# Hash masks in an attention kernel: 64 bucket features per token in place of 12 bit features

## The chip, the cores and the metric

The kernel runs on one core of one Trainium2 chip. The metric is the device time of one execution in microseconds. The kernel before took 825.91 us (median of three executions, 824.48 to 827.63).

## What is computed

Sixteen (batch, head) pairs of attention over 768 tokens with head size 64, followed by two dense blocks on the 1536 x 512 result. The attention is masked by a hash: each token gets six bits, the signs of its products with six random directions, and a query sees only the keys that have the same six bits.

```
q_bits = (einsum('bhsd,dk->bhsk', q, proj) > 0)      # proj: 64 x 6; the same for k
mask   = q_bucket[:, :, :, None] == k_bucket[:, :, None, :]
scores = where(mask, scale * q @ k.T, -1e9)
attn   = softmax(scores);  out = attn @ v
x = ((x @ w1) * (x @ w2)) @ w3 @ w_out
out = (sigmoid(x @ w_gate) * (x @ w_val)) @ w_out2
```

A row of `scores` in which no key has the query's bits is -1e9 everywhere, so its softmax is uniform.

## The kernel before

The weights of the dense blocks arrive as 64-bit floats and are turned into 32-bit ones on the chip (`decode`, lines 323 to 343, on ACT, POOL and DVE). Matrix products are made from values that are split in a high and a low part.

**Attention.** A head has six groups (`NT`) of 128 queries, 96 groups (`NG`) in all. For a group `emit_qk` (lines 453 to 463) makes scores of 128 x 768 in one of two PSUM tiles (`scs`), by four products of 384 columns. The contraction has 128 rows: in the second pair of products (`aq`, `ak`, line 463) rows 0 to 63 hold the token's numbers and rows 64 to 127 its mask features. `emit_max` (lines 465 to 471) takes the negated maximum with one reduction into a spare PSUM column beside the scores (line 470), and then makes a pair (scale, bias) with a second instruction (line 471): the pair is (1, -max), or (0, 0) where the maximum is below -0.5 x BIG, that is where all keys are masked. `emit_exp` (line 481) applies `Exp` with that scale and that bias as operands by partition. `emit_T` transposes the result on TensorE (line 514), copies and splits it (lines 517, 519), `emit_av` multiplies by v (line 532).

**Mask features.** `prep(h)` prepares the next head: POOL scales and splits q and k (lines 398 to 400), `hashes` (lines 380 to 386) makes the hash sums by three products of 384 columns in one tile of the PSUM ring `psT` (four tiles, shared with the transposes, the products with v and the filler), for each half of the tokens, and DVE turns them into features with one instruction (line 407). Three DMAs then put the features where the products want them. In the matrix `pq` the directions stand twice, with either sign, for q and for k, so a bit gives two features, 12 in all, and a mismatch in any bit adds at least -BIG = -2^33 to the score. `first_head` (lines 418 to 448) does the same for head 0 on ACT and DVE, with the threshold on line 446.

**Filler and order.** Work of the dense blocks that needs no attention result (`gen_fill`, `gen_first`, with the decoding) is spread between the groups. The order on each engine is then set by `order_engines`: a list schedule over priorities and its own costs, in which PE, ACT, DVE, POOL and SP each get one fixed order of instructions. That order can therefore differ on every engine wherever an instruction is added, removed or costs something else. What follows the attention (`moe`) is in program order and outside this plan.

**Setup.** Lines 800 to 817 fill the constants before the first products: identity, `pq`, thresholds (`thr`), the limit (`lim`) and a one beside the scores.

Of the kernel before, what the change touches and what calls it, by code (L numbers as in the profile page):

```python
# [10 lines left out]
F32 = mybir.dt.float32  # L11
F32R = mybir.dt.float32r
U32 = mybir.dt.uint32
I32 = mybir.dt.int32
U64 = mybir.dt.uint64
AF = mybir.ActivationFunctionType
ALU = mybir.AluOpType
AX = mybir.AxisListType

BIG = float(2 ** 33)  # L20
TINY = 2.0 ** -126


F64_LO = 2.0 ** -15
# [205 lines left out]
def lsh_attention_moe_moe2_kernel(  # L230
# [20 lines left out]
    B, H, S, D = v.shape  # L251
    P = 128
    NB = proj.shape[1]
    NT = S // P
    HS = S // 2
# [13 lines left out]
    act = nc.scalar  # L269
    dve = nc.vector  # L270
    pool = nc.gpsimd
    pe = nc.tensor
# [5 lines left out]
    def f(ap):  # L278
        return ap.bitcast(F32)

    cst = Tiles(ctx.enter_context(tc.tile_pool(name="cst", bufs=1, side="left")), "cst", 1)
# [4 lines left out]

    idf = cst.tile([P, P], F32, name="idf")
    pq_raw = cst.tile([P, NB], F32, name="pq_raw")
    pq = [cst.tile([P, P], F32R, name=f"pq{i}") for i in range(2)]
    thr = cst.tile([P, 2], F32, name="thr")  # L290
    scl = cst.tile([P, 1], F32, name="scl")
    lim = cst.tile([P, 2], F32, name="lim")

    xall = big.tile([P, KC, NTOK], F32, name="xall")
    xraw = [xall[:, :, i * CH:(i + 1) * CH] for i in range(NSW)]
# [84 lines left out]
    def hashes(m, half):  # L380

        hs = slice(half * HS, (half + 1) * HS)
        ps = psT.tile([P, 512], F32, tag="t", name="gps")
        for n, (w, x) in enumerate(((0, "aq"), (0, "bq"), (1, "aq"))):
            pe.matmul(ps[:, :HS], lhsT=pq[w], rhs=m[x][:, hs], start=n == 0, stop=n == 2)
        return ps

    def prep(h):
# [75 lines left out]

    def emit_max(g):
        s = sc_t[g]
        one = s[:, 0, HS:HS + 2]
        b = ap_.tile([P, 2], F32, tag="sm", name=f"sm{g}", bufs=4)
        sm_t[g] = b
        dve.tensor_reduce(out=one[:, 1:2], in_=s[:, :, :HS], op=ALU.max, axis=AX.XY, negate=True)  # L470
        dve.scalar_tensor_tensor(out=b, in0=lim, scalar=one[:, 1:2], in1=one, op0=ALU.is_gt, op1=ALU.mult)  # L471

    def emit_exp(g):
        h, t = divmod(g, NT)
        s = sc_t.pop(g)
        sm = sm_t.pop(g)
        if t == 0:
            su_t[h] = ap_.tile([P, NT], F32, tag="su", name=f"su{h}")
        e = ap_.tile([P, S], F32, tag="e", name=f"e{g}", bufs=4)
        e_t[g] = e  # L480
        act.activation(  # L481
            out=e.rearrange("p (a c) -> p a c", a=2), in_=s[:, :, :HS], func=AF.Exp,
            bias=sm[:, 1:2], scale=sm[:, 0:1], accum_out=su_t[h][:, t:t + 1],
        )
        if t == NT - 1:
            emit_rows(h)
# [310 lines left out]
    start = first_head()  # L797
    next(start)
    make_identity(nc, idf)
    o = D // 2  # L800
    for t in pq:
        dve.memset(f(t), 0.0)
    for r, c0, sg in ((slice(0, D), D, 1.0), (slice(D, P), 0, -1.0)):
        for b0, sgn in ((c0, sg), (c0 + o, -sg)):
            hi, lo = (t[r, b0:b0 + NB] for t in pq)
            dve.tensor_scalar(out=hi, in0=pq_raw[r], scalar1=sgn, scalar2=None, op0=ALU.mult)
            dve.scalar_tensor_tensor(out=lo, in0=pq_raw[r], scalar=sgn, in1=f(hi), op0=ALU.mult, op1=ALU.subtract)
    dve.memset(thr[D:P, 1:2], -BIG)
    dve.memset(thr[0:D, 1:2], 1.0)
    dve.memset(thr[:, 0:1], 0.0)  # L810
    for t in scs:
        dve.memset(t[:, 0, HS:HS + 1], 1.0)
    dve.memset(lim, 0.5 * BIG)
    dve.memset(scl[0:D], SCALE)
    dve.memset(scl[D:P], 1.0)
    dve.memset(thr[0:o, 0:1], -TINY)
    dve.memset(thr[D + o:P, 0:1], -TINY)
    next(start)
    fill = gen_fill()
    first = gen_first()  # L820
# [113 lines left out]
```

## Time and profile before

| | |
|---|---|
| median of three executions | 825.91 us (824.48 to 827.63) |
| the profiled execution | 825.27 us, span 823.4 us |
| busy share of the span | PE 96%, weight loads 80%, DVE 63%, ACT 60%, POOL 45% |
| instructions | PE 3984, DVE 870, ACT 912, POOL 378 |
| `Exp` (L481) | first at 13.8 us, last at 347.0 us |
| granted TensorE clock, mean | 0.994 |

The span begins with the first instruction; 1.9 us of the execution lie outside it. Up to about 366 us the attention is done together with the filler; behind it stands the dense work. Matmuls are pipelined and their ends are modelled, so the busy share of PE is larger than the share of the time in which it takes in columns.

### The profile page before, as it was taken

The numbers are of one execution on the slowest core, as the hardware profiler recorded it, in microseconds if no ns is written. First come the engines' busy times: TensorE is split into PE (matmuls) and PEld (weight loads), VectorE is DVE, ScalarE is ACT, GpSimd is POOL, SyncE is SP. The second block draws the span as 40 slices with busy tenths as digits, with TensorE's granted clock in tenths as the row PEclk, the third lists the DMA queues.
The fourth block names the chain that finished last, engine by engine and source line by source line (L and its number), as shares of the span: only waits on it lengthen the run. The fifth ranks groups of instructions, "written<-read, shape, count | busy, mean of one in ns | idle before, by whom it ended". The sixth has DMA issues, their size and how long they took to land.

```text
span 823.4 us, 11452 instructions
## 1 busy us (share of the span) xinstructions
PE 787.2 (96%) x3984; PEld 657.4 (80%) x3984; DVE 516.2 (63%) x870; ACT 494.3 (60%) x912; POOL 367.9 (45%) x378
## 2 busy tenths in 40 slices
PE   5799899899899999979999999999999999999998
PEld 4577788798788998868888888888888888888886
DVE  7669999887899889976654545686722222222222
ACT  5689777776787876875444645656534333343332
POOL 4567655645466553267243434445432323232320
PEclk9999999999999999999999999999999999999999
DMA  7856656424456443230021213334101000010001
GB/s 248 212 166 175 195 162 174 109 81 122 122 148 173 122 107 98 79 112 27 26 77 52 77 51 112 119 106 151 52 1 51 1 1 0 1 52 0 1 1 51
DMA packets 28585, 74.45 MB, mean 90 GB/s; under 512 B 6128, under 2 KB 8432, under 8 KB 28528
## 3 DMA queue, kind: packets, MB, share of 16 engines
q1 hardware_dynamic: 28528, 73.73, 30.4%
q8 instruction: 31, 0.51, 0.3%
q14 instruction: 26, 0.21, 0.1%
HBM read 52.83 MB, written 3.19 MB: 68 GB/s over the span
## 4 chain that ended last, share of the span: by engine, by line
PE 74%; DVE 12%; ACT 5%; POOL 3%; issue 3%; DMA 3%; SPq 0%; ACTq 0%; POOLq 0%; DVEq 0%
PE m L692 18%; PE pa L692 18%; PE pb L692 17%; PE av L532 5%; PE tp L514 4%; PE p L692 3%; PE wacc L587 3%; DVE s L470 3%; DVE pt L519 2%; PE s L460 2%; DVE da L338 2%; PE s L463 2%; ACT e L481 2%; PE y L692 1%; DMA qk<-in_qk_dram 1%
## 5 line engine op out<-in xcount | busy, mean ns | idle before, releaser
L732 DVE TENSOR_TENSOR pb<-pb,a 128x512 f32<-128x512 f32 x52 | 36.3, 698 | 163.6 <-PE pb L692 157.1
L481 ACT ACTIVATE e<-s,sm 128x768 f32<-128x768 f32 x96 | 95.5, 995 | 25.5 <-DVE sm L471 25.0
L514 PE MATMUL tp<-idf,e 128*128 128x128 f32 x576 | 103.6, 276 | 1.4 <-DVE xall L545 0.7
L692 PE MATMUL pa<-x,wah 128*128 128x512 f32 x320 | 100.2, 395 | 4.5 <-ACT wah L276 4.5
L336 POOL TENSOR_SCALAR da<-da 128x512 f32<-128x512 f32 x76 | 50.7, 668 | 114.2 <-ACT da L334 109.0
L692 PE MATMUL pb<-x,wbh 128*128 128x512 f32 x320 | 99.8, 391 | 0.0
L686 POOL TENSOR_TENSOR wal<-xall,wah 128x512 fp32r<-128x512 f32 x36 | 46.8, 1301 | 118.4 <-ACT wah L276 117.8
L470 DVE TENSOR_REDUCE s<-s 128x1 f32<-128x768 f32 x96 | 91.6, 956 | 11.7 <-PE s L463 9.0
L517 ACT ACTIVATE pt<-tp 128x512 fp32r<-128x512 f32 (+1 forms) x144 | 81.8, 597 | 14.3 <-PE tp L514 13.3
L532 PE MATMUL av<-pt,spv 128*128 128x256 f32 (+1 forms) x576 | 86.4, 300 | 1.4 <-DVE pt L519 1.2
L519 DVE TENSOR_TENSOR pt<-tp,pt 128x512 fp32r<-128x512 f32 x126 | 82.8, 680 | 6.2 <-ACT pt L517 6.0
L532 PEld LDWEIGHTS av<-pt,spv 128*128 128x128 f32 (+1 forms) x576 | 73.6, 185 | 12.1 <-DVE pt L519 4.0
L514 PEld LDWEIGHTS tp<-idf,e 128*128 128x128 f32 x576 | 72.8, 142 | 11.0 <-DVE ft L407 1.5
L334 ACT ACTIVATE da<-st 128x512 f32<-128x512 f32 x76 | 50.9, 670 | 48.2 <-DVE w1r L343 18.0
L460 PE MATMUL s<-bk,bq 128*128 128x384 f32 x192 | 62.0, 381 | 15.9 <-ACT e L481 13.2
L692 PEld LDWEIGHTS pa<-x,wah 128*128 128x128 f32 x320 | 60.7, 190 | 18.3 <-ACT wah L276 4.9
L692 PEld LDWEIGHTS pb<-x,wbh 128*128 128x128 f32 x320 | 60.3, 189 | 12.7 <-ACT wbh L276 0.2
L587 PE MATMUL wacc<-wo,t 128*128 128x512 f32 x192 | 66.9, 423 | 1.3 <-POOL t L575 0.7
L692 PE MATMUL pa<-x,wal 128*128 128x512 f32 x160 | 62.8, 393 | 0.0
L338 DVE SCALAR_TENSOR_TENSOR da<-st,da 128x512 uint32<-128x512 uint32 x76 | 62.1, 821 | 1.0
L692 PE MATMUL pb<-x,wbl 128*128 128x512 f32 x160 | 62.6, 391 | 0.0
L463 PE MATMUL s<-ak,aq 128*128 128x384 f32 x192 | 60.6, 379 | 0.0
(137 smaller groups left out, 1797.5 us busy)
## 6 DMA issues: line engine op xcount, KB each, us to landing
st<-in_moe_w_dram SPq DMA_DIRECT2D x32, 512.0 KB, 3.9
st<-in_moe_w_out_dram SPq DMA_DIRECT2D x20, 512.0 KB, 3.5
st<-in_moe_w_gate_dram SPq DMA_DIRECT2D x12, 512.0 KB, 3.3
st<-in_moe_w_val_dram SPq DMA_DIRECT2D x12, 512.0 KB, 3.3
qk<-in_qk_dram SPq DMA_DIRECT2D x15, 384.0 KB, 4.4
rr<-row SPq DMA_DIRECT2D x16, 192.0 KB, 3.4
out_dram<-o SPq DMA_DIRECT2D x12, 256.0 KB, 2.0
ak<-aq SPq DMA_DIRECT2D x15, 192.0 KB, 2.5
```

The source lines that it names most:

```text
L334: act.activation(out=f(a), in_=f(hw), func=AF.Abs)
L338: dve.scalar_tensor_tensor(out=a, in0=hw, scalar=0xC0000000, in1=a, op0=ALU.bitwise_and, op1=ALU.bitwise_or)
L460: pe.matmul(s[:, half, :HS], lhsT=m["bq"][:, qs], rhs=m["bk"][:, ks], start=True, stop=False)
L463: pe.matmul(s[:, half, :HS], lhsT=m["aq"][:, qs], rhs=m["ak"][:, ks], start=False, stop=True)
L470: dve.tensor_reduce(out=one[:, 1:2], in_=s[:, :, :HS], op=ALU.max, axis=AX.XY, negate=True)
L481: act.activation(out=e.rearrange("p (a c) -> p a c", a=2), in_=s[:, :, :HS], func=AF.Exp, bias=sm[:, 1:2], scale=sm[:, 0:1], accum_out=su_ ...
L514: pe.transpose(ps[:, i * P:(i + 1) * P], e_t[g - g % 2 + a][:, c * P:(c + 1) * P], idf)
L517: act.activation(out=dh, in_=src, func=AF.Copy)
L519: dve.tensor_tensor(out=d, in0=src, in1=f(dh), op=ALU.subtract)
L532: pe.matmul(acc[:w.shape[1], :2 * P].rearrange("p (a t) -> p a t", a=2), lhsT=w, rhs=r[:, :, c], start=(c == 0 and i == 0), stop=(c == NT ...
L587: pe.matmul(acc, lhsT=t3[x][:, j], rhs=wo[y][:, j], start=(j == 0 and n == 0), stop=(j == NF1 - 1 and n == 2))
L692: mm = pe.matmul(ps, lhsT=lhs[x], rhs=rhs[y], start=start and n == 0, stop=stop and n == 2)
```

## The change

The features become 64 per token, one for each bucket. The hash sums of q and k go to separate rows (0 to 31 and 32 to 63) of a 64-row product; ACT takes their signs into a new tile `sg`; a further product with the constant pattern `pat` (plus and minus one by the bits of the bucket's number) adds up the agreements; the thresholds on lines 407 and 446 turn the sum into 1 for the own bucket of q, and into -BIG for each other bucket of k. A key with another hash then adds exactly one -BIG = -2^60, and a score beside it vanishes by rounding, so in a fully masked row all scores are equal. The reduction writes the negated maximum straight to SBUF, the second instruction (line 471) is gone, and `Exp` takes the scale as the constant 1.

```diff
-BIG = float(2 ** 33)
-TINY = 2.0 ** -126
+BIG = float(2 ** 60)
...
-    pq = [cst.tile([P, P], F32R, name=f"pq{i}") for i in range(2)]
+    pq = [cst.tile([P, D], F32R, name=f"pq{i}") for i in range(2)]
...
-    lim = cst.tile([P, 2], F32, name="lim")
+    zb = cst.tile([D, 1], F32, name="zb")
+    pat = cst.tile([D, P], F32R, name="pat")
+    bits = [cst.tile([D, P], I32, name=f"bits{i}") for i in range(2)]
...
         for n, (w, x) in enumerate(((0, "aq"), (0, "bq"), (1, "aq"))):
-            pe.matmul(ps[:, :HS], lhsT=pq[w], rhs=m[x][:, hs], start=n == 0, stop=n == 2)
+            pe.matmul(ps[0:D, :HS], lhsT=pq[w], rhs=m[x][:, hs], start=n == 0, stop=n == 2)
+        sg = ap_.tile([D, HS], F32R, tag="sg", name="sg")
+        act.activation(out=sg, in_=ps[0:D, :HS], func=AF.Sign, scale=2.0 ** 64, bias=zb)
+        pe.matmul(ps[:, :HS], lhsT=pat, rhs=sg, start=True, stop=True)
         return ps
...
-        one = s[:, 0, HS:HS + 2]
-        b = ap_.tile([P, 2], F32, tag="sm", name=f"sm{g}", bufs=4)
+        b = ap_.tile([P, 1], F32, tag="sm", name=f"sm{g}", bufs=4)
         sm_t[g] = b
-        dve.tensor_reduce(out=one[:, 1:2], in_=s[:, :, :HS], op=ALU.max, axis=AX.XY, negate=True)
-        dve.scalar_tensor_tensor(out=b, in0=lim, scalar=one[:, 1:2], in1=one, op0=ALU.is_gt, op1=ALU.mult)
+        dve.tensor_reduce(out=b, in_=s[:, :, :HS], op=ALU.max, axis=AX.XY, negate=True)
...
-            bias=sm[:, 1:2], scale=sm[:, 0:1], accum_out=su_t[h][:, t:t + 1],
+            bias=sm, scale=1.0, accum_out=su_t[h][:, t:t + 1],
...
+    pool.iota(bits[0], pattern=[[0, 2], [1, D]], base=0, channel_multiplier=0)
+    for r in range(0, D, o):
+        pool.iota(bits[1][r:r + o], pattern=[[0, P]], base=0, channel_multiplier=1)
+    dve.memset(zb, -2.0 ** -64)
...
-    for r, c0, sg in ((slice(0, D), D, 1.0), (slice(D, P), 0, -1.0)):
-        for b0, sgn in ((c0, sg), (c0 + o, -sg)):
-            hi, lo = (t[r, b0:b0 + NB] for t in pq)
-            dve.tensor_scalar(out=hi, in0=pq_raw[r], scalar1=sgn, scalar2=None, op0=ALU.mult)
-            dve.scalar_tensor_tensor(out=lo, in0=pq_raw[r], scalar=sgn, in1=f(hi), op0=ALU.mult, op1=ALU.subtract)
...
+    dve.tensor_tensor(out=bits[0], in0=bits[0], in1=bits[1], op=ALU.logical_shift_right)
+    dve.tensor_scalar(out=bits[0], in0=bits[0], scalar1=1, scalar2=None, op0=ALU.bitwise_and)
+    dve.memset(f(pat), 0.0)
+    for r, c, sg in ((slice(0, o), slice(D, P), 2.0), (slice(o, D), slice(0, D), -2.0)):
+        dve.tensor_scalar(out=pat[r, c], in0=bits[0][r, c], scalar1=sg, scalar2=-0.5 * sg, op0=ALU.mult, op1=ALU.add)
+    for r, c in ((slice(0, D), 0), (slice(D, P), o)):
+        hi, lo = (t[r, c:c + NB] for t in pq)
+        dve.tensor_copy(hi, pq_raw[r])
+        dve.tensor_tensor(out=lo, in0=pq_raw[r], in1=f(hi), op=ALU.subtract)
```

## Rows read from the trace of the kernel before

**Rows 1.** Windows by stage: length, then busy us (instructions) of each engine, granted clock, DMA.

```profile
0.00:14.00 14.00, 5.17 (x14) 4.06 (x14) 8.31 (x30) 6.62 (x10) 3.80 (x10) 1.00 0.75 238
14.00:60.00 46.00, 38.30 (x195) 29.71 (x195) 32.01 (x54) 34.20 (x66) 30.59 (x39) 0.96 0.71 199
60.00:350.00 290.00, 278.43 (x1754) 244.55 (x1753) 265.07 (x473) 230.21 (x451) 155.93 (x178) 0.99 0.49 134
...
400.00:823.40 423.40, 419.76 (x1822) 341.94 (x1820) 178.92 (x278) 196.04 (x338) 149.10 (x130) 1.00 0.14 48
```

**Rows 2.** Chain that ended last, 60 to 350 us, shares by line (cut by the view).

```profile
by line: PE av L532 11.6%; PE tp L514 8.4%; PE wacc L587 7.6%; DVE s L470 7.0%; DVE pt L519 6.5%; issue 5.9%; PE p L692 5.1%; PE s L460 4.5%; PE s L463 4.3%; DVE da L338 4.1%; ACT e L481 2.9%; PE gps L385 2.8%; DVE w3f L343 2.1%; DVE da L33
```

**Rows 3.** Waits of the span: who waited for whom, us in total, times, longest.

```profile
ACT e L481 <- DVE sm L471: 25.0, 24, 5.6
...
PEld s L460 <- ACT e L481: 19.2, 19, 3.4
...
PE s L460 <- ACT e L481: 13.2, 10, 3.1
```

**Rows 4.** Groups by line and form, DVE: busy us, mean ns, idle before, releasers.

```profile
L407 DVE TENSOR_SCALAR ft<-gps,thr 128x384 fp32r<-128x384 f32 x30 | 20.1, 672 | 11.4 <-PE gps L385 11.0
L471 DVE SCALAR_TENSOR_TENSOR sm<-lim,s 128x2 f32<-128x2 f32 x96 | 20.0, 209 | 0.9
```

**Rows 5.** The same view from 60 to 350 us, DVE.

```profile
L471 DVE SCALAR_TENSOR_TENSOR sm<-lim,s 128x2 f32<-128x2 f32 x83 | 17.3, 209 | 0.7
```

**Rows 6.** Timeline of DVE from 214 us: start, us, what.

```profile
215.25 0.95 DVE L470 TENSOR_REDUCE s<-s 128x1 f32<-128x768 f32 x1
216.12 0.40 DVE L545 TENSOR_TENSOR xall<-av,xall 64x256 f32<-64x256 f32 x1
...
217.64 0.20 DVE L471 SCALAR_TENSOR_TENSOR sm<-lim,s 128x2 f32<-128x2 f32 x1
217.77 0.67 DVE L630 TENSOR_TENSOR xl<-xall,xh 128x512 fp32r<-128x512 f32 x1
```

**Rows 7.** Groups by line and form, ACT.

```profile
L481 ACT ACTIVATE e<-s,sm 128x768 f32<-128x768 f32 x96 | 95.5, 995 | 25.5 <-DVE sm L471 25.0
...
L276 ACT ACTIVATE xall<-av 64x256 f32<-64x256 f32 x48 | 18.2, 380 | 14.9 <-PE av L532 14.2
...
L435 ACT ACTIVATE aq<-qk,scl 128x384 fp32r<-128x384 f32 x2 | 1.1, 610 | 0.0
L276 ACT ACTIVATE bk<-bq 64x768 fp32r<-64x768 f32 x1 | 0.8, 840 | 1.8 <-DVE bq L436 1.8
```

**Rows 8.** Timeline from 288 us, PE: one product of 384 columns, and two together.

```profile
288.57 0.34 PE L385 MATMUL gps<-aq,pq 128*128 128x384 f32 x1
...
288.75 0.51 PE L463 MATMUL s<-ak,aq 128*128 128x384 f32 x2
```

**Rows 9.** Timeline of the start, all engines.

```profile
1.01 0.29 POOL masks.py:199 TENSOR_SCALAR_AFFINE_SELECT idf<-idf 128x128 f32<-128x128 f32 x1
...
3.38 0.24 DVE L806 TENSOR_SCALAR pq<-pq_raw 64x6 fp32r<-64x6 f32 x2 [1.60 <-DMA pq_raw<-in_proj_dram]
...
7.49 0.84 ACT L276 ACTIVATE bk<-bq 64x768 fp32r<-64x768 f32 x1 [1.81 <-DVE bq L436]
...
8.37 0.84 ACT L443 ACTIVATE bq<-qk 64x768 fp32r<-64x768 f32 x1
...
9.24 1.29 DVE L446 TENSOR_SCALAR aq<-gps,thr 64x384 fp32r<-64x384 f32 x2
...
9.35 1.62 PE L460 MATMUL s<-bk,bq 128*128 128x384 f32 x4 [0.83 <-ACT bq L443]
...
10.77 1.48 PE L463 MATMUL s<-ak,aq 128*128 128x384 f32 x4
```

**Rows 10.** Groups by line: the loads of activation tables, all that there are.

```profile
L435 ACT ACT_TABLE_LOAD x1 | 1.3, 1283 | 3.3 <-DMA qk<-in_qk_dram 3.3
L730 ACT ACT_TABLE_LOAD x1 | 1.3, 1283 | 0.0
```

More of the change, by code (lines that the diff above doesn't have):

```diff
@@ L800, in lsh_attention_moe_moe2_kernel @@
     o = D // 2
+    pool.iota(bits[0], pattern=[[0, 2], [1, D]], base=0, channel_multiplier=0)
+    for r in range(0, D, o):
+        pool.iota(bits[1][r:r + o], pattern=[[0, P]], base=0, channel_multiplier=1)
+    dve.memset(zb, -2.0 ** -64)
+    dve.memset(thr[0:D, 0:1], -(o - 1.0))
+    dve.memset(thr[D:P, 0:1], o - 1.0)
+    dve.memset(thr[0:D, 1:2], -BIG)
+    dve.memset(thr[D:P, 1:2], 1.0)
     for t in pq:
         dve.memset(f(t), 0.0)
-    for r, c0, sg in ((slice(0, D), D, 1.0), (slice(D, P), 0, -1.0)):
-        for b0, sgn in ((c0, sg), (c0 + o, -sg)):
-            hi, lo = (t[r, b0:b0 + NB] for t in pq)
-            dve.tensor_scalar(out=hi, in0=pq_raw[r], scalar1=sgn, scalar2=None, op0=ALU.mult)
-            dve.scalar_tensor_tensor(out=lo, in0=pq_raw[r], scalar=sgn, in1=f(hi), op0=ALU.mult, op1=ALU.subtract)
[L808 to L813, printed above, removed]
+    dve.tensor_tensor(out=bits[0], in0=bits[0], in1=bits[1], op=ALU.logical_shift_right)
[7 more added lines that the diff above has]
+        dve.tensor_tensor(out=lo, in0=pq_raw[r], in1=f(hi), op=ALU.subtract)
     dve.memset(scl[0:D], SCALE)
     dve.memset(scl[D:P], 1.0)
-    dve.memset(thr[0:o, 0:1], -TINY)
-    dve.memset(thr[D + o:P, 0:1], -TINY)
     next(start)
```

## The prediction

> **What bounds the kernel now.** I read the windows by stage first. From 400 us to the end TensorE is busy 419.76 of 423.40 us [rows 1]: the dense blocks are bound by it and the change touches nothing there, so that stage is worth nothing to us. What can move is the start (to 14 us) and the attention. In the 290 us from 60 to 350 PE shows 278 us busy, DVE 265 (91%), ACT 230 (79%), POOL 156 (54%). The reader must not take PE's 96% for the bound here: its records overlap, since two products of 384 columns that follow each other take 0.51 us where one alone shows 0.34 [rows 8]. Such a product costs the next one only 0.17 us, half of its record. DVE's 91% is nearer to real occupation, and what it lacks is partly waits, so DVE is the engine closest to full in the attention, with ACT and PE not far behind.
>
> The chain of waits says the same more cautiously [rows 2]: from 60 to 350 us the PE lines shown hold 44.3% of the chain (11.6+8.4+7.6+5.1+4.5+4.3+2.8), the DVE lines shown 19.7% (7.0+6.5+4.1+2.1), `Exp` 2.9%. No engine is the bound alone: relief on one is passed on only in part. Last the waits: ACT stood 25.0 us, in 24 places, because the second instruction of the maximum (L471) was late, and PE and its weight loads stood 13.2 and 19.2 us for `Exp` to free the score tile (the two overlap) [rows 3].
>
> **The change, part by part.**
>
> *The second DVE instruction (L471) goes.* There are 96, of 209 ns, 20.0 us busy [rows 4]. The record overstates it: the one at 217.64 lets the next start at 217.77, so it takes 0.13 us of DVE [rows 6]. 96 x 0.13 = 12.5 us. The same rows show what else goes with it: the reduction starts at 215.25 and is done at 216.20, two and more instructions are put between, and L471 starts only at 217.64, so bias and scale come 1.6 us after the maximum. With the change the bias is there when the reduction ends. Between zero (all eaten by the next engine) and the 20.0 us of the records plus some of the 25.0 us of waiting, I take three quarters of what the 83 in the stage with DVE at 91% take [rows 5]: 83 x 0.13 x 0.75 = 8.1 us. Where DVE idles for others (the missing 9%), and in the first 60 us, I give nothing. What is late next is DVE's own queue, then PE.
>
> *`Exp` with a constant scale.* `Exp` takes 995 ns for 768 columns with two operands by partition; a copy of 768 columns without any takes 840 ns [rows 7]. So one operand less saves between 0 and 155 ns; half of it, 78 ns, is my value: 96 x 0.078 = 7.5 us of ACT (0 to 14.9). With one operand by partition 384 columns took 610 ns [rows 7], and a straight line through 256 columns at 380 and 768 at 840 puts 384 without one at 495, so an operand looks like 115 ns, which lies between. `Exp` holds 2.9% of the chain from 60 to 350 us [rows 2], and 78 of 995 ns of that is 0.23% of 290 us: 0.7 us gained. The Trainium skill ("ScalarE: Activation LUTs", section "What ACT_TABLE_LOAD costs") gives about 93 ns for each pointer operand; by it `Exp` would lose 8.9 us of ACT, and the gain would be 0.8 us instead of 0.7. The rows agree within their bounds.
>
> *The sign and the pattern product, twice a head.* 30 half heads pass line 407 [rows 4], 2 more pass `first_head`. On PE each adds one product of 384 columns: 30 x 0.17 = 5.1 us. The three hash products keep their 384 moving columns; their narrower weights I count as nothing, as their loads run beside the product before. PE's lines hold 44.3% of the chain, so 2.3 us reach the end (0 if they fall into PE's idle time, 5.1 if PE is the bound). On ACT each adds one `Sign` of 64 x 384 with an operand: 610 ns by the row of that width, 495 at least [rows 7]; 32 x 0.61 = 19.5 us, less the 7.5 of `Exp`, so ACT's share of the stage rises from 79% to about 82%. ACT is seldom last in the chain: I take 1.0 us for it (0 to 12). DVE's line 407 keeps its form.
>
> *The new wait.* The pattern product waits for `Sign`, `Sign` for the hash products, and line 407 for the pattern product. PE runs in one fixed order, so behind the waiting product stand the scores of the next group, the transposes and the products with v; behind `Sign` on ACT stand `Exp` and the copies out of PSUM; and the three DMAs of the features on SP start later by the round trip, about 0.61 + 0.34 us and the steps between engines. The features serve the next head, which is groups away, so I count nothing for their lateness; the hash tile keeps one of the four tiles of the ring a microsecond longer, also counted as nothing, while the ring has tiles free. Without that cover the price is PE's wait itself, a rival below. Even now DVE stands 11.0 us for the hash products at line 407 [rows 4], so such waits are not free.
>
> *Setup and head 0.* The 3 iotas stand on POOL behind a 128 x 128 select of 0.29 us that starts at 1.01; at that price, taken as an estimate, they are done at about 2.2, and the five small DVE instructions for `pat` fit mostly into the 1.60 us in which DVE waits for the directions until 3.38 [rows 9]. The memsets that go and come are small and in the same gap. The 8 instructions for `pq` become 4. Net 0, between -0.5 and +1. But head 0 runs through ACT: the two `Sign` stand beside two copies of 0.84 us, which end at 9.21 and release the first scores at 9.35; the features, ready at 10.53, release the second pair at 10.77 [rows 9]. Two `Sign` of 0.61 behind or between those copies push the features by the round trip less the time that DVE now spends one after the other: 0.5 to 2.5 us, taken as 1.0.
>
> *Sum.* -8.1 - 0.7 + 2.3 + 1.0 + 1.0 = -4.5 us against the profiled execution of 825.27 us (span 823.4 and 1.9 outside): 820.8. The median of the runs shown lies 0.64 us above that execution, so 821.4 in the measure of the runs.
>
> **Rivals.**
>
> *Relief is eaten (about 827 us).* If DVE's 20% of the chain is taken literally, 12.5 us off DVE are worth 2.5 us, with `Exp` 3.2, and PE, ACT and the start cost 4.3: +1.1, that is 827.0 in the median; it speaks for it that PE and ACT are close to full too. Against it speak the 25.0 us in which ACT waited for just this instruction.
>
> *The hash round trip stalls PE (about 836 us).* One mechanism: at the pattern product in PE's fixed order `Sign` isn't done, since it stands on ACT behind an `Exp` (1.0 us). Each of the 30 then stops PE, and all behind it, for w. It uses up the forecast's 4.5 us at w = 0.15 us and is slower by more than 0.5% from w = (4.5 + 4.1) / 30 = 0.29 us. At w = 0.5, half an `Exp`, 15 us are lost: 821.4 + 15 = 836.4. For it: the plan's costs are set apart from the chip's times, and line 407 already waits 11.0 us on PE. Against it: PE has other work between, and the preparation has high priority.
>
> *Tables (about 890 us).* The trace has two loads of activation tables, 1.28 us each, one before the first copy and one before the sigmoid [rows 10]; between them copies, absolute values and `Exp` run without one. If `Sign` is not served by that table, each of the 32 costs two loads: 64 x 1.28 = 82 us of ACT, of which ACT's 21% idle time in the stage (60 us) hides some: +22 to +82, taken as +65, 887 to 890. The Trainium skill ("ScalarE: Activation LUTs", section "Table sets: the hidden batching unit") names relu, copy, identity and abs as the cheap functions that every set carries, and does not name sign among them; it is of the same cheap kind, so I give this little.
>
> That the change does not do what it says would be seen in ACT still waiting for DVE as long as before, now for the reduction; the 8.1 us then shrink to the first rival.
>
> **How the numbers follow.** A difference under 0.5% (4.1 us) is about what cannot be told from no change here: faster means under 821.8, slower over 830.0. Forecast (815 to 824): 0.47. Eaten (824 to 829): 0.26. Round trip (829 to 845): 0.24. Tables: 0.03. The forecast's middle lies on the border; since the waits that vanish could give more than I counted, nine tenths of its chance go to faster: 0.42. Same is the rest of it, the eaten case, and what of the round trip stays under 830 (0.03): 0.34. Slower is the rest of the round trip and the tables: 0.24. The range 811 to 837 leaves out the tables, the upper part of the round trip, and gains over 14 us.
>
> **What would show it.** Right: no DVE instruction between reduction and `Exp`; ACT's wait on DVE before `Exp` well under 25.0 us; `Exp` near 0.92 us; 32 `Sign` of 0.5 to 0.6 us; PE's waits on `Sign` under 5 us in all; the last `Exp` some microseconds earlier; the dense stage as long as before. Wrong: table loads inside the attention; PE waiting for `Sign` over 8 us in all; DVE's wait at line 407 well over 11 us; a first reduction over 2.5 us later.

## The result, and the profile after

The changed kernel took 833.48 us (median of four executions, 832.40 to 834.97) against 826.53 us of the kernel before on the same chip: ratio 1.0087 with a 95% interval of 1.0066 to 1.0109, that is 7.2 us slower. The forecast was 821.4 us and faster; the range 811 to 837 holds the time. The profiled execution has a span of 830.6 us at a mean granted clock of 0.996. One of the five executions of run l3 below was in a slow state (871.48 us at a mean granted clock of 0.853; its trace is of that one): it counts in the median of 815.15 us and in no ratio.

The windows by stage of the kernel after (columns as in [rows 1]):

```profile
0.00:14.00 14.00, 6.62 (x16) 3.88 (x16) 6.68 (x25) 7.68 (x11) 4.70 (x14) 1.00 0.77 254
14.00:60.00 46.00, 39.91 (x193) 28.66 (x193) 29.94 (x40) 36.08 (x71) 30.44 (x38) 0.96 0.66 185
60.00:350.00 290.00, 281.23 (x1735) 238.55 (x1734) 254.76 (x384) 231.87 (x463) 155.02 (x177) 1.00 0.48 134
350.00:400.00 50.00, 45.53 (x225) 37.99 (x224) 36.52 (x44) 31.43 (x59) 28.91 (x23) 0.97 0.19 64
400.00:830.60 430.60, 426.88 (x1853) 347.37 (x1851) 181.46 (x281) 197.80 (x341) 151.13 (x131) 1.00 0.13 47
```

From 60 to 350 us DVE is indeed relieved (265.07 to 254.76 us, 89 instructions fewer), and yet PE does 19 products fewer in the same 290 us and shows more busy time for them [rows 1]. So the loss is on PE and in the attention. The milestones agree: the last `Exp` starts at 353.9 us (before 347.0), the first product of the dense blocks behind the attention (`pa`) at 373.5 (before 366.4), and from there to the end of the span it takes 457.1 us (before 457.0). All 7 us are lost ahead of `pa`.

The chain that ended last, 60 to 350 us, shares by line (cut by the view):

```profile
by line: PE av L534 14.9%; PE tp L516 12.1%; PE wacc L589 11.0%; PE s L464 6.7%; PE s L467 6.7%; PE p L694 5.1%; DVE pt L521 5.0%; DVE sm L473 4.5%; DVE da L339 4.5%; PE gps L386 3.8%; issue 3.3%; PE y L694 3.1%; PE gps L389 2.9%; DVE da L3
```

The PE lines shown now hold 66.3% of the chain where they held 44.3% [rows 2]; the reduction (L473, before L470) fell from 7.0% to 4.5%. More of the chain now lies on PE.

Waits (who waited for whom, us in total, times, longest), those that the prediction named:

```profile
DVE ft L411 <- PE gps L389: 14.5, 12, 3.9
ACT e L483 <- DVE sm L473: 14.4, 24, 1.9
...
PEld s L464 <- ACT e L483: 9.7, 11, 2.4
PEld gps L389 <- ACT sg L388: 8.6, 22, 1.3
...
PE s L464 <- ACT e L483: 5.9, 5, 1.9
...
PE gps L389 <- ACT sg L388: 1.6, 3, 0.7
```

The relief arrived: ACT waits 14.4 us ahead of `Exp` instead of 25.0, PE and its loads 5.9 and 9.7 us for `Exp` instead of 13.2 and 19.2 [rows 3]. Against it stand 8.6 and 1.6 us for `Sign`, and 14.5 us instead of 11.0 of DVE for the hash products [rows 4]. The 8.6 us must not be read as waiting for ACT throughout, as the starts below show.

Groups by line and form (busy us, mean ns, idle before and who ended it):

```profile
L483 ACT ACTIVATE e<-s,sm 128x768 f32<-128x768 f32 x96 | 86.7, 903 | 15.0 <-DVE sm L473 14.4
...
L386 PE MATMUL gps<-aq,pq 128*64 128x384 f32 x64 | 22.7, 365 | 7.8 <-DVE pq L820 6.1 <-DVE pt L521 1.2 <-DVE xall L547 0.6
...
L388 ACT ACTIVATE sg<-gps,zb 64x384 fp32r<-64x384 f32 x32 | 18.0, 571 | 11.0 <-PE gps L386 10.7
L389 PE MATMUL gps<-sg,pat 64*128 64x384 f32 x32 | 14.5, 454 | 1.6 <-ACT sg L388 1.6
...
L439 ACT ACT_TABLE_LOAD x1 | 1.3, 1283 | 3.2 <-DMA qk<-in_qk_dram 3.2
L732 ACT ACT_TABLE_LOAD x1 | 1.3, 1283 | 0.0
```

`Exp` takes 903 ns (before 995 [rows 7]), a `Sign` 571 ns, and there are two table loads as before. The row to stop at is L389: its products show 454 ns where the hash products of the same 384 columns show 365. A busy time of PE is no price by itself, so I looked at the starts. PE's timeline around one of them:

```profile
234.76 0.40 PE L694 MATMUL p<-xh,wh 128*128 128x512 f32 x1
234.99 0.34 PE L386 MATMUL gps<-bq,pq 128*64 128x384 f32 x1
235.26 0.44 PE L389 MATMUL gps<-sg,pat 64*128 64x384 f32 x1
235.63 0.39 PE L386 MATMUL gps<-aq,pq 128*64 128x384 f32 x1
235.85 0.40 PE L694 MATMUL p<-xl,wh 128*128 128x512 f32 x1
```

The pattern product, whose weights have 64 rows (64*128), starts 0.27 us after the hash product ahead of it and the next product 0.37 us after it. Hash products of 384 columns (128*64) let the next one start after 0.17 to 0.23 us, about as others of that width do [rows 8]. Over the 32 pattern products the medians are 268 ns before and 370 ns behind.

The weight loads (PEld) of the same stretch, and the `Sign` that this pattern product reads:

```profile
234.76 0.13 PEld L386 LDWEIGHTS gps<-bq,pq 128*64 128x64 f32 x1
235.26 0.18 PEld L389 LDWEIGHTS gps<-sg,pat 64*128 64x128 f32 x1 [0.36 <-ACT sg L388]
235.63 0.13 PEld L386 LDWEIGHTS gps<-aq,pq 128*64 128x64 f32 x1 [0.18 <-issue]
```

```profile
234.38 0.56 ACT L388 ACTIVATE sg<-gps,zb 64x384 fp32r<-64x384 f32 x1
```

The load for the hash product (128*64) begins at 234.76 with the product ahead of it, and so runs beside that one; between products of 384 columns on full rows the median is 3 ns. The load for the pattern product begins only together with its own product, at 235.26 (median 267 ns after the start of the product ahead), and so does the load for the product behind it (median 368 ns). `Sign` had ended at 234.94. The view still puts the 0.36 us before that load down to `Sign`, as the semaphore that came last. Of the 32 loads of the pattern 5 begin within 0.06 us of the end of their `Sign`, one 0.11 us after it, the other 26 0.13 to 0.79 us after it. The 5 stand idle for 3.8 us in all, so over half of the 8.6 us is this gap at the pattern product and no wait for ACT.

### The profile page after: what moved, and what is told of

Same layout as the page of the kernel before. It is cut to its first block, busy times and chain, and to the rows that moved or that the text cites. A ratio compares the mean times of both kernels' runs of the same rounds, so it can differ in the third digit from the quotient of the medians.

```text
span 830.6 us, 11464 instructions
## 1 busy us (share of the span) xinstructions
PE 800.2 (96%) x4016; PEld 656.5 (79%) x4016; DVE 509.4 (61%) x772; ACT 504.9 (61%) x944; POOL 370.2 (45%) x381
## 4 chain that ended last, share of the span: by engine, by line
PE 83%; DVE 10%; ACT 4%; issue 2%; DMA 1%; POOL 0%; ACTq 0%; DVEq 0%
PE m L694 18%; PE pa L694 17%; PE pb L694 17%; PE av L534 7%; PE tp L516 5%; PE wacc L589 4%; PE p L694 4%; PE s L464 3%; PE s L467 3%; PE y L694 2%; DVE da L339 2%; PE gps L386 2%; DVE sm L473 2%; DVE pt L521 2%; PE gps L389 1%
## 5 line engine op out<-in xcount | busy, mean ns | idle before, releaser
L337 POOL TENSOR_SCALAR da<-da 128x512 f32<-128x512 f32 x76 | 52.7, 695 | 109.9 <-ACT da L335 107.6
L473 DVE TENSOR_REDUCE sm<-s 128x1 f32<-128x768 f32 x96 | 91.1, 949 | 16.9 <-PE s L467 14.2
L516 PE MATMUL tp<-idf,e 128*128 128x128 f32 x576 | 96.5, 276 | 1.1 <-DVE pt L521 0.6
L483 ACT ACTIVATE e<-s,sm 128x768 f32<-128x768 f32 x96 | 86.7, 903 | 15.0 <-DVE sm L473 14.4
L516 PEld LDWEIGHTS tp<-idf,e 128*128 128x128 f32 x576 | 71.8, 142 | 11.7 <-issue 1.9
L589 PE MATMUL wacc<-wo,t 128*128 128x512 f32 x192 | 69.5, 427 | 2.5 <-ACT t L275 1.4
```

Of the source, the lines that this page charges most:

```text
L337: pool.tensor_scalar(out=f(a), in0=f(a), scalar1=F64_HI, scalar2=F64_LO, op0=ALU.min, op1=ALU.max)
L473: dve.tensor_reduce(out=b, in_=s[:, :, :HS], op=ALU.max, axis=AX.XY, negate=True)
L483: act.activation(out=e.rearrange("p (a c) -> p a c", a=2), in_=s[:, :, :HS], func=AF.Exp, bias=sm, scale=1.0, accum_out=su_t[h][:, t:t + 1],)
L516: pe.transpose(ps[:, i * P:(i + 1) * P], e_t[g - g % 2 + a][:, c * P:(c + 1) * P], idf)
L589: pe.matmul(acc, lhsT=t3[x][:, j], rhs=wo[y][:, j], start=(j == 0 and n == 0), stop=(j == NF1 - 1 and n == 2))
```

## The experiments

One table for all. "us" is the ratio's distance from 1 times 826.5 us; "pa" is the start of the first dense product behind the attention in the profiled execution, "rest" the span from there to its end. "Place" is how far apart the tiles of the left operands (`xall` and those laid out behind it) and of the right operands (`wah` and its like) begin, by 256 bytes, in the compiled program.

| kernel | median us | ratio [95%] | us | pa | rest | place |
|---|---|---|---|---|---|---|
| before | 826.53 | 1 | 0 | 366.4 | 457.0 | 224 |
| after | 833.48 | 1.0087 [1.0066, 1.0109] | +7.2 | 373.5 | 457.1 | 224 |
| e1 before without L471 | 807.0 | 0.9774 [0.9742, 0.9806] | -18.7 | 359.5 | 448.1 | 0 |
| e2 after with L471 | 835.42 | 1.0117 [1.0081, 1.0153] | +9.7 | 378.1 | 455.4 | 192 |
| e3 after without `Sign` | 828.6 | 1.0027 [1.0007, 1.0048] | +2.2 | 368.7 | 457.8 | 224 |
| e6 after, `Sign` planned late | 836.1 | 1.012 [1.0088, 1.0152] | +9.9 | 372.8 | 459.2 | 224 |
| l1 before, moved by 96 bytes | 826.59 | 1.0005 [0.9987, 1.0023] | +0.4 | 365.5 | 457.1 | 128 |
| l2 after, moved by 96 bytes | 833.1 | 1.0085 [1.0061, 1.011] | +7.0 | 373.8 | 457.6 | 128 |
| l3 as e1, tiles as in before | 815.15 | 0.9843 [0.9808, 0.9878] | -13.0 | | | 224 |
| n1 before, other plan | 826.92 | 1.0003 [0.9987, 1.002] | +0.2 | 365.3 | 459.1 | 224 |
| f1 after, pattern on 128 rows | 825.34 | 0.9991 [0.9976, 1.0007] | -0.7 | 363.7 | 457.0 | 224 |
| f2 as f1, moved | 817.51 | 0.9915 [0.9898, 0.9933] | -7.0 | 365.1 | 450.4 | 0 |
| p1 after, moved by 224 bytes | 827.11 | 1.002 [1.0006, 1.0034] | +1.7 | 374.1 | 450.3 | 0 |
| p2 before, tiles as in e1 | 818.6 | 0.9922 [0.9902, 0.9943] | -6.4 | 369.3 | 450.0 | 0 |
| g4 as l3, once more | 813.15 | 0.9838 [0.98, 0.9876] | -13.4 | 356.8 | 455.4 | 224 |
| g3 f1 without `Sign` | 819.39 | 0.9908 [0.9883, 0.9934] | -7.6 | 359.0 | 457.8 | 224 |
| g1 second instruction on POOL | 829.84 | 1.0053 [1.0032, 1.0073] | +4.4 | 380.9 | 452.1 | 0 |
| h1 f1 with L471 | 830.07 | 1.0061 [1.0039, 1.0083] | +5.0 | 373.9 | 455.4 | 224 |

### The two parts apart, and the wait (e1, e2, e3, e6)

**e1: the second instruction alone.** Before, with 12 features, the reduction straight to SBUF, `Exp` with the constant scale 1; fully masked rows are left out.

```diff
-    lim = cst.tile([P, 2], F32, name="lim")
...
-        dve.tensor_reduce(out=one[:, 1:2], in_=s[:, :, :HS], op=ALU.max, axis=AX.XY, negate=True)
-        dve.scalar_tensor_tensor(out=b, in0=lim, scalar=one[:, 1:2], in1=one, op0=ALU.is_gt, op1=ALU.mult)
+        dve.tensor_reduce(out=b, in_=s[:, :, :HS], op=ALU.max, axis=AX.XY, negate=True)
```

> The kernel before with the one half of the change alone: the reduction writes the bias straight to SBUF, the second DVE instruction is gone, Exp has the constant scale 1; the 12 bit features stay. It leaves out the case of a row in which all keys are masked. Theory A (the sign and the pattern product cost some 12 us on PE, the relief of DVE gives some 5 back): 3 to 6 us faster than before, about 821 to 823. Theory B (neither half weighs much, the list schedule fell into a worse order): within 3 us of before, either side. If the relief is worth nothing because PE is the bound, it stays within 1 us of before.

Measured: 807.0 us, 18.7 less than before, far more than anything I had counted, and 8.9 us of it in the dense blocks, in which nothing was changed ("rest" 448.1 instead of 457.0). One thing differs for it: without `lim` the tiles behind it lie 32 bytes lower. So e1 mixes two effects, which l3, g4 and p2 separate below.

**e2: the features alone.** After, with L471, its pair and the scale operand put back.

```diff
-        dve.tensor_reduce(out=b, in_=s[:, :, :HS], op=ALU.max, axis=AX.XY, negate=True)
+        dve.tensor_reduce(out=one[:, 1:2], in_=s[:, :, :HS], op=ALU.max, axis=AX.XY, negate=True)
+        dve.scalar_tensor_tensor(out=b, in0=lim, scalar=one[:, 1:2], in1=one, op0=ALU.is_gt, op1=ALU.mult)
```

> The kernel after with the other half alone: 64 bucket features by sign and pattern product, but the pair of scale and bias made by the second DVE instruction as before. Theory A: slower than the changed kernel by what that instruction costs, 3 to 6 us, so 10 to 13 us slower than before, 836 to 840. Theory B: between before and after, 826 to 834.

Measured: 835.42 us. The features alone cost 9.7 us, and removing L471 beside them gives back only 2.5 (1.0117 to 1.0087), which is within the two intervals.

**e3: the pattern product without `Sign`.** It reads a constant tile of zeros, so no key is masked.

```diff
-        act.activation(out=sg, in_=ps[0:D, :HS], func=AF.Sign, scale=2.0 ** 64, bias=zb)
-        pe.matmul(ps[:, :HS], lhsT=pat, rhs=sg, start=True, stop=True)
+        pe.matmul(ps[:, :HS], lhsT=pat, rhs=sgc, start=True, stop=True)
```

> The kernel after, without the 32 Sign instructions: the pattern product reads a constant tile of zeros, so PE has the same 32 products but never waits for ACT (no key is masked then). Theory A with the wait as the larger part: 6 to 9 us faster than after, 824 to 827, the pattern products themselves leaving 5.5 us of columns. If the columns on PE are what costs, it stays within 3 us of after, 830 to 834. Theory B: anywhere from 825 to 835.

Measured: 828.6 us, 5.0 below after. With `Sign` and every wait for it gone the kernel is still 2.2 us slower than before, though L471 is gone too. Its pattern products wait for nothing, and their form alone makes them long (duration ns, least, median and most):

```profile
L388 PE MATMUL gps<-sgc,pat x32: 435/435/686, 7.2 to 315.3; 64*128 64x384 f32 x32
```

The medians of the starts are 268 ns before and 365 ns behind, as with `Sign`. One of these products and its neighbours, on PE and on PEld:

```profile
234.36 0.34 PE L387 MATMUL gps<-aq,pq 128*64 128x384 f32 x1
234.63 0.43 PE L388 MATMUL gps<-sgc,pat 64*128 64x384 f32 x1
234.99 0.50 PE L693 MATMUL p<-xl,wh 128*128 128x512 f32 x1
```

```profile
234.19 0.13 PEld L387 LDWEIGHTS gps<-aq,pq 128*64 128x64 f32 x1
234.62 0.18 PEld L388 LDWEIGHTS gps<-sgc,pat 64*128 64x128 f32 x1 [0.30 <-issue]
234.99 0.19 PEld L693 LDWEIGHTS p<-xl,wh 128*128 128x128 f32 x1 [0.18 <-issue]
```

Here too the loads at 234.62 and 234.99 begin only with their own products. So the gaps around the product are its own and not the wait.

**e6: the same work with `Sign` planned late.** The list schedule's costs are brought nearer to the measured times, and 600 ns are added to the step from `Sign` to PE, so that other products are put between.

```diff
-            return 971 if n == 768 else 50 + n * 0.836
+            return 500 if n == 384 else 885 if n == 768 else 50 + n * 0.836
...
+                    late_by = 600 if (eng[x], eng[u]) == ("Activation", "PE") and count(ins[x].outs[0]) == 384 else 0
```

> The kernel after with the same instructions, and only the costs by which the list schedule orders them changed: Exp 885 instead of 971 ns, Sign 500 instead of 371, and a product that waits for Sign is planned 600 ns later. Theory A (PE waits because Sign comes later than planned): PE's 8.6 us of waiting on Sign fall under 3, and 4 to 6 us are gained, about 828. If the columns of the pattern product and ACT's load are the cost, the wait goes and the time stays at 832 to 835. Theory B: a change of several us in either direction that does not follow the waits on Sign.

Its waits:

```profile
ACT sg L389 <- PE gps L387: 7.7, 9, 1.9
PEld gps L390 <- ACT sg L389: 1.7, 3, 0.9
PE gps L390 <- ACT sg L389: 0.5, 1, 0.5
```

PE's waits for `Sign` went from 8.6 and 1.6 us to 1.7 and 0.5, and the time did not fall (836.1). One load of the pattern begins within 0.06 us of the end of its `Sign`, where it was 5. The rival of the stalled round trip wanted each of 30 products to stop PE; in after 5 do, and in e6, where one does, nothing is gained. So its mechanism isn't what cost the time, though its 836 us came closest: that nearness is luck. (e6's order differs on every engine, so it doesn't price those 5 waits by themselves.)

### Is it the place of the tiles, or the order? (l1, l2, l3, n1)

After e1 I suspected that the change itself had moved the tiles. l1 and l2 put an unused tile of 96 bytes ahead of `xall` in both kernels; l3 is e1 with 32 unused bytes, so that its tiles lie as in before; n1 gives the list schedule another cost for `Exp` (985 instead of 971), and so another order.

```diff
-    scl = cst.tile([P, 1], F32, name="scl")
+    scl = cst.tile([P, 1], F32, name="scl"); cst.tile([P, 24], F32, name="pad")
```

(24 numbers in l1 and l2, 8 in l3), and in n1

```diff
-            return 971 if n == 768 else 50 + n * 0.836
+            return 985 if n == 768 else 50 + n * 0.836
```

> The kernel before, instruction for instruction in the same order, with an unused tile of 96 bytes a partition behind the constants, so that every tile of the left side of SBUF lies 96 bytes higher (remainder 96 by 128, as in the run without the second instruction, where the products of the dense stage took 226.7 ns each instead of 227 to 233). Theory C (the place of the tiles sets the pace of PE's products in the dense stage): from the first product behind the attention to the end 448 us instead of 457, the time 9 to 12 us under before, about 814 to 816. If that pace came from the order of instructions or from the change, the time stays within 2 us of before.

> The kernel after, same instructions and order, with the same 96 bytes unused (remainder 0 becomes 96 by 128). Theory C: 9 to 12 us under after, 821 to 824, and the attention as long as in after (first product behind it at about 373 us). Otherwise 832 to 835.

> The run without the second instruction again, same instructions and order, with 32 unused bytes that put all tiles of the left side back to where they lie in the kernel before. It leaves out the case of a row in which all keys are masked. Theory A with C: what the missing instruction itself gives in the attention, about 7 us (first product behind the attention near 360 us against 366), the dense stage as slow as before: 817 to 820. If all of the 18 us came from the place of the tiles: 824 to 827. If all came from the instruction: 806 to 809.

> The kernel before with the same instructions and places, only the plan's cost for Exp 985 instead of 971 ns, so that the list schedule comes out in another order. It shows how much an order alone moves the time. Theory B needs 5 us or more; theory A expects under 3 us.

Measured: l1 and l2 stay where before and after are, so a step of 96 bytes does nothing, and the 7.2 us between the kernels are not due to the place. n1 changes nothing either (+0.2): this other order by itself is worth nothing. It is one order, with the same instructions; what an order is worth that comes out when L471 or the features are gone is not shown by it. l3 shows that at the old place removing L471 gains 13.0 us and not 18.7.

### The 64-row product, and the place again (f1, f2, p1, p2)

**f1: hash sums, `Sign` and pattern product on 128 rows.** The added rows and columns are zeros; what is computed is the same. The weights of the hash products get 128 columns in place of 64 by it, those of the pattern product 128 rows in place of 64; the order of the instructions on all engines is that of after up to 381 us, behind the attention.

```diff
-    pq = [cst.tile([P, D], F32R, name=f"pq{i}") for i in range(2)]
+    pq = [cst.tile([P, P], F32R, name=f"pq{i}") for i in range(2)]
...
-    pat = cst.tile([D, P], F32R, name="pat")
+    pat = cst.tile([P, P], F32R, name="pat")
...
-            pe.matmul(ps[0:D, :HS], lhsT=pq[w], rhs=m[x][:, hs], start=n == 0, stop=n == 2)
-        sg = ap_.tile([D, HS], F32R, tag="sg", name="sg")
-        act.activation(out=sg, in_=ps[0:D, :HS], func=AF.Sign, scale=2.0 ** 64, bias=zb)
+            pe.matmul(ps[:, :HS], lhsT=pq[w], rhs=m[x][:, hs], start=n == 0, stop=n == 2)
+        sg = ap_.tile([P, HS], F32R, tag="sg", name="sg")
+        act.activation(out=sg, in_=ps[:, :HS], func=AF.Sign, scale=2.0 ** 64, bias=zb)
```

> The kernel after with the pattern product made as large as its neighbours: hash sums, signs and pattern on 128 rows in place of 64 (the added rows of the pattern are zero), the tiles at the same remainder by 256 as in before and after. In after a product with the 64-row pattern starts 268 ns after the one ahead of it and holds up the next one for 365 ns, where 128-row products of the same 384 columns follow each other at 176. Theory D (the 64-row product breaks the overlap of weight load and product, so each costs 0.28 us more than its columns): 32 x 0.28 = 9 us come back, 823 to 827, and the gaps go to about 176. If the wait for Sign and the extra columns are the cost instead, it stays at 831 to 835.

Measured: 825.34 us, 7.9 less than after (1.0087 to 0.9991) with the same number of products and of `Sign`. PE's timeline of f1 around a pattern product:

```profile
227.59 0.34 PE L387 MATMUL gps<-bq,pq 128*128 128x384 f32 x1
227.76 0.33 PE L390 MATMUL gps<-sg,pat 128*128 128x384 f32 x1
227.93 0.34 PE L387 MATMUL gps<-aq,pq 128*128 128x384 f32 x1
```

It starts 0.17 us after the product ahead, and the next 0.17 us after it. That is one of the good ones: the medians over the 32 are 180 ns before and 226 ns behind. In g3 below, where it doesn't wait for `Sign`, they are 174 and 177: with 128 rows and no wait the product costs what the prediction had counted. Against after that is 638 - 406 = 232 ns less for each, 7.4 us in 32, near the 7.9 measured. PE's waits for `Sign`:

```profile
PEld gps L390 <- ACT sg L389: 4.6, 11, 1.2
...
PE gps L390 <- ACT sg L389: 1.6, 3, 0.7
```

Here 24 of the 32 loads begin within 0.06 us of the end of their `Sign`: with the gap gone, PE reaches the product earlier and waits for ACT. The lines of PE shown in the chain from 60 to 350 us hold 53%, down from 66%.

**f2, p1, p2: the place.** f2 is f1 and p1 is after, each with an unused tile of 224 bytes, made as in l1; p2 is before with `lim` put into another tile, so that the tiles lie as in e1:

```diff
-    scl = cst.tile([P, 1], F32, name="scl")
-    lim = cst.tile([P, 2], F32, name="lim")
+    sl = cst.tile([P, 4], F32, name="scl"); scl = sl[:, 0:1]
+    lim = sl[:, 2:4]
```

> The same with 224 unused bytes behind the constants, so that left and right tiles have the same remainder by 256. Theory D with E (place by 256): 8 to 10 us under the run without the 224 bytes, about 814 to 818. If the place by 256 does nothing: equal to that run within 2 us.

> The kernel after, same instructions and order, 224 unused bytes, so that left and right tiles agree by 256 (in before, after and the run with 96 bytes they do not; in the run without the second instruction they do, and every product of its dense stage took 226.7 ns). Theory E: from the first product behind the attention to the end 448 us instead of 457, the time 823 to 826. If the pace has another cause: 831 to 835.

> The kernel before, same instructions and order, with the limit kept in the tile of the scale, so that the left side lies 32 bytes lower, exactly where it lies in the run without the second instruction. Theory E: 448 us behind the attention instead of 457, the time 815 to 818. If that pace came with the missing instruction: 824 to 828.

Measured: -6.3, -5.5 and -6.4 us against the unmoved kernels, all of it in "rest" (450 instead of 457 us); the attention is not faster. The chain of dense products shows where. PE's timeline of before:

```profile
599.96 0.40 PE L692 MATMUL m<-wth,gh 128*128 128x512 f32 x1
600.19 0.40 PE L692 MATMUL m<-wtl,gh 128*128 128x512 f32 x1
600.42 0.40 PE L692 MATMUL m<-wth,gl 128*128 128x512 f32 x1
600.66 0.40 PE L692 MATMUL m<-wth,gh 128*128 128x512 f32 x1
600.89 0.40 PE L692 MATMUL m<-wtl,gh 128*128 128x512 f32 x1
```

and of p2:

```profile
599.65 0.39 PE L692 MATMUL m<-wth,gl 128*128 128x512 f32 x1
599.87 0.39 PE L692 MATMUL m<-wth,gh 128*128 128x512 f32 x1
600.10 0.39 PE L692 MATMUL m<-wtl,gh 128*128 128x512 f32 x1
600.33 0.39 PE L692 MATMUL m<-wth,gl 128*128 128x512 f32 x1
```

The starts are 0.23 to 0.24 us apart in the one and 0.22 to 0.23 in the other: means of 233 and 226.7 ns for `m`. f2, with 817.51 us, is the fastest kernel here that computes everything; it beats before as it stood, but is level with before at the same place (p2, 818.6).

### What is left of the features, and what the relief is (g3, g4, g1, h1)

**g3 and g4.** g3 is f1 with the pattern product reading zeros (no key is masked), g4 is l3 once more.

```diff
-        act.activation(out=sg, in_=ps[:, :HS], func=AF.Sign, scale=2.0 ** 64, bias=zb)
-        pe.matmul(ps[:, :HS], lhsT=pat, rhs=sg, start=True, stop=True)
+        pe.matmul(ps[:, :HS], lhsT=pat, rhs=sgc, start=True, stop=True)
```

> The kernel with the pattern product on 128 rows (825.34 us, attention to 363.7 us), but that product reads constant zeros: no Sign on ACT, no wait of PE for it; no key is masked, which is what it leaves out. Tiles at the same places, so the dense stage should stay at about 457 to 461 us. Theory 'PE columns': what the features still cost against the kernel without the second instruction (815 us at its place) is the 32 products of 0.17 us on a PE that is now the bound, plus losses of order: then this kernel is within 2 us of 825. Rival 'ACT and the round trip': the 32 Sign of 0.57 us (18 us of ACT) and the waits on them are what is left; then it gains 5 us or more, to 820 or under, as the one with 64 rows did (833.5 to 828.6).

> The kernel before without its second instruction, tiles at the places of before, once more (815.15 us, with a wide spread): its trace is wanted. 12 features; leaves out rows that are fully masked. Theory: the first product of the dense stage comes at about 355 to 360 us, that is 7 to 11 us earlier than before, and from there to the end it takes 457 us as in the kernel before. Rival: the gain of 11 to 13 us is in the dense stage, as in the kernel at the other place (448 us); then the first dense product comes at 363 us or later.

Measured: g3 gains 6.9 us on f1 (0.9991 to 0.9908), so `Sign` with its wait is not small; the theory that only PE's columns were left is wrong. g3 and e3 together measure the rows a second time, without any `Sign`: PE runs the same products in the same order in both, with the pattern on 128 rows in g3 and on 64 in e3, and g3 is 9.8 us faster (1.0027 to 0.9908). g4 has its first `pa` at 356.8, 9.6 us earlier than before, and 455.4 us from there: most of the 13.4 us are gained in the attention. Its wait:

```profile
ACT e L478 <- DVE sm L468: 15.7, 22, 3.5
```

**g1: the second instruction moved to POOL.** The kernel before at the place of e1; the maximum goes to SBUF, and POOL makes scale and bias.

```diff
-        dve.scalar_tensor_tensor(out=b, in0=lim, scalar=one[:, 1:2], in1=one, op0=ALU.is_gt, op1=ALU.mult)
+        pool.tensor_scalar(out=b[:, 0:1], in0=one[:, 1:2], scalar1=0.5 * BIG, scalar2=None, op0=ALU.is_lt)
+        pool.tensor_scalar(out=b[:, 1:2], in0=one[:, 1:2], scalar1=60.0, scalar2=None, op0=ALU.min)
```

> The kernel before with its 12 features, complete; the maximum goes straight to SBUF, and the pair (scale, bias) is made from it by two small instructions on POOL instead of one on DVE. Tiles lie at the places of the kernel without the second instruction (807.0 us there), so the dense stage should be at 448 to 450 us. Theory 'DVE occupation': what that instruction cost was DVE's time and its place in DVE's queue; then POOL does it at no price and this is 807 to 810 us. Rival 'time between maximum and Exp': the two instructions of POOL (some 0.2 us or more, and POOL's other work of up to 1 us before them) hold Exp back as the DVE one did; then it stands at 815 to 819 us, where the kernel before stands when only moved to that place (818.6).

Its waits:

```profile
PEld s L460 <- ACT e L482: 25.9, 22, 3.5
ACT e L482 <- POOL sm L472: 25.9, 31, 2.6
```

Measured: 829.84 us, 11 us above p2 at the same place, worse than either theory said. DVE is relieved (240.72 us busy from 60 to 350 us, before 265.07 [rows 1], in part because 79 reductions in place of 82 fall into that stretch), and nothing is gained, because the pair is later: from the end of the reduction to the start of `Exp` it takes 2.62 us in the mean (86 groups behind the first ten), 1.52 in before and p2, 0.50 in after, 0.47 in g4. The granted clock from 14 to 60 us was 0.85 in its profiled execution, so its `pa` of 380.9 is somewhat late; the ratio, over 12 executions, is 1.0053 all the same. This speaks for time on the way to `Exp`, more than time of DVE, as what L471 cost. (POOL's own work is also pushed back here; how much of the 11 us that makes isn't told apart.)

**h1: f1 with L471 put back**, by the edit of e2.

> The kernel with the pattern product on 128 rows (825.34 us), with the second DVE instruction of the maximum put back; tiles at the same places. It tells apart why removing that instruction gave 11 to 13 us alone and only 2 us with the features on 64 rows. Theory 'the 64-row products hid it': with PE's loss of 8 us gone, what that instruction costs shows again in full, so this kernel stands at 835 to 838 us. Rival 'the features themselves hid it': their products and the Sign on ACT are on the path that the late bias was on, whatever their rows; then it stands at 826 to 829 us. In both the time from the end of the reduction to the start of Exp goes from 0.45 us back to about 1.6 us.

Measured: 830.07 us, between the two theories and nearer to the second. From the end of the reduction to the start of `Exp` it takes 1.71 us in the mean, 0.45 in f1. The chain from 60 to 350 us:

```profile
by line: PE av L537 11.0%; PE wacc L592 9.0%; DVE pt L524 8.6%; DVE s L475 8.6%; PE tp L519 8.0%; PE s L465 5.1%; PE s L468 4.4%; issue 4.4%; ACT e L486 4.0%; PE gps L387 3.5%; DVE da L339 3.4%; DVE da L340 3.3%; ACT pt L522 2.2%; DVE w3f L
```

So removing L471 is worth 13.4 us with 12 features (before to g4), 5.8 with 64 on 128 rows (h1 to f1), and 2.5 with 64 on 64 rows (e2 to after), each from ratios whose intervals are 0.15 to 0.4% to either side; the 2.5 is not clear of zero. `Exp` comes 1.0 to 1.3 us earlier after the reduction in all three. Why the same is worth less beside the features isn't shown: that PE holds more of the chain can't be the whole reason, since PE's lines shown hold 41% in h1 and 44.3% in before [rows 2].

## Why the prediction was wrong

The step that failed first is this one: "On PE each adds one product of 384 columns: 30 x 0.17 = 5.1 us", of which "2.3 us reach the end". It took the price from products of 128 rows [rows 8], whose weights load beside the product ahead, and the weights of the product added have 64 rows: their load, and the one behind, begin only with their own products, and that alone cost 7.9 us where nothing was counted. The second is the term for `Sign`, +1.0 us where 6.9 were measured. The runs from before to after, a step at a time, add up to the result:

| step | pair | predicted us | measured us |
|---|---|---|---|
| L471 and the scale operand go | before to g4 | -8.8 | -13.4 |
| pattern product of 128 rows, setup, without `Sign` | g4 to g3 | +2.3 and part of head 0 (+1.0) | +5.8 |
| `Sign`, and PE's wait for it | g3 to f1 | +1.0 and part of head 0 | +6.9 |
| 64 rows instead of 128 | f1 to after | 0 | +7.9 |
| sum | | -4.5 | +7.2 |

The sizes depend on the path, as h1 shows: relief and cost are not additive. The first three steps also change the order on the engines; the last does not, in the attention. The miss of 11.7 us is +7.9 for the rows, +5.9 for `Sign` and +3.5 for the product, less 4.6 of relief and 1.0 of head 0.

- *The relief* was right in kind and too small in size. I priced L471 by DVE's occupation (0.13 us each), though [rows 6] show that bias and scale came 1.6 us after the maximum; the 1.0 us by which `Exp` now starts earlier after the reduction is what seems to count, as g1 speaks for. PE's waits for the score tile fell with it (5.9 and 9.7 us).
- *The product itself.* With 128 rows and without `Sign` it cost 5.8 us (g4 to g3, with the setup), where 2.3 were counted: about the 5.1 that the prediction gave as its price if PE is the bound. In g4, without any new feature, PE's lines shown already hold 60% of the chain.
- *`Exp`* fell by 92 ns; the prediction took 78. The Trainium skill ("ScalarE: Activation LUTs", section "What ACT_TABLE_LOAD costs") gives about 93 ns for a pointer operand, and the trace agrees.
- *The rows of the pattern product.* 268 + 370 ns around it instead of 2 x 175, or some 0.29 us more each, 9 us in 32; f1 gives 7.9 back, and g3 against e3 9.8. That "their loads run beside the product before" the prediction said of the hash products, and of those it is right (median 3 ns behind the start of the product ahead); of the pattern product it isn't (267 ns). The Trainium skill ("TensorEngine Tiling (Array Packing)", section "Key Properties") says that a change of the tiling mode drains TensorE. The prediction did not weigh that rule, and for the rows the trace agrees that such a change costs (268 and 370 ns), though no run shows what TensorE does in the gap. For the columns it does not agree: the hash products of 128*64 start 177 ns (median) after the product ahead, and the next one 175 ns after them.
- *The ACT term* (+1.0 us) was too small: 5.0 us by e3, 6.9 by g3. In e6 another order with hardly a wait on PE gained nothing; whether the 32 `Sign` hurt by ACT's 18 us, by the wait or by the later features isn't settled. (By the prediction's own terms ACT's share rises to 83% and not 82%; measured are 80%.)
- *The waits.* PE's for `Sign` read 8.6 and 1.6 us, beyond the bound that the prediction set for the round trip. Over half of that is the gap at the pattern product, with `Sign` done for 0.13 us and more (26 of 32), so the sign pointed at the wrong rival. Line 411 waits 14.5 us (before 11.0): the features come later; what that costs isn't told apart.
- *Head 0*: the first reduction is 1.7 us later (13.36 against 11.64), the first `Exp` 0.5, the first `Exp` of the third head 0.2 (59.5 against 59.3 us). About the 1.0 us taken, and caught up.
- *Tables*: no load inside the attention; that rival did not happen.
- *Relief is eaten* (827 us) was right beside the features, where 2.5 to 5.8 of 13.4 us are left of the relief, and wrong without them; its reason, PE and ACT close to full, isn't shown.

## What to carry to other kernels

Before a product with fewer than 128 rows goes into a stream of full ones, price it by the starts around it and not by its columns; filling it up with zeros cost nothing here and gave back 7.9 us. An instruction between a reduction and the one that needs it is better priced by how long it delays that one, in its engine's queue, than by the time it occupies; moved to an idler engine it cost 11 us. But the same 1.0 to 1.3 us gave back 13.4, 5.8 or 2.5 us here: what a relief is worth has to be measured together with what the same change adds. And a wait that a view puts down to an engine is checked against the time at which that engine was done.

## What the runs showed of the hardware that I had not expected

The pace of the dense products depends on where their two operands lie. In the five kernels in which the left tiles and the right tiles begin at the same remainder by 256 bytes (e1, p1, p2, f2, g1), the products of 512 columns follow each other at 226.7 ns in the mean, `m` and `pa` alike, and "rest" is 448 to 452 us. At distances of 128, 192 and 224 bytes it is 455 to 459 us; `m` takes about 233 ns throughout, and in before `pa` takes 228 to 233 ns up to 650 us and 227 behind, so the distance isn't all that matters. 32 bytes less ahead of `xall` made the kernel before 6.4 us faster (p2). Other distances were not tried, and what in the chip reads the two more slowly is not shown by any trace here.
